# Routing attention with a hard-swish feed-forward: 32x32 block turns on VectorE for the sorted pairs

## Chip, core and metric

One Trainium2 chip, one core. The metric is device time in microseconds of one launch. All engines work on their own instruction streams and wait for each other through semaphores: TensorE (PE: matmuls and transposes by matmul), VectorE (DVE), ScalarE (ACT), GpSimd (POOL, which here also issues the gathers and scatters by row index) and SyncE (SP, which issues most transfers). Each engine runs its stream strictly in order, so an instruction that waits holds everything behind it on its engine.

## What is computed

```python
q_assign = argmax(q_n . c_n)          # per token and head, 16 clusters
k_assign = argmax(k_n . c_n)
mask = q_assign[:, :, :, None] == k_assign[:, :, None, :]
scores = scale * matmul(q, k.T);  scores = where(mask, scores, -1e9)
attn = softmax(scores);  x = matmul(attn, v)          # (4, 8, 768, 64)
x = x.transpose(0, 2, 1, 3).reshape(3072, 512)
h = x @ w_in                                          # 512 -> 2048
out = (h * clip(h + 3, 0, 6) / 6) @ w_out             # 2048 -> 512
```

Everything is float32; 4 batches, 8 heads, 768 tokens, head dimension 64.

## The kernel before, in words

Heads are handled in pairs, 16 of them (`NPAIR`), four to a batch. Pairs 0 to 6 take the plain way: all 768x768 scores with a mask added by a matmul. While they run, the weights are loaded and decoded by ACT and DVE, and the first eight items of the feed-forward are slipped in at the steps listed in `up_at`. Two steps `n` (a double step) are done per turn of that loop. The first feed-forward block needs `divide(0, 0)` (L529 to L533): the attention output `xb` times the reciprocal row sums `rb`, both fetched from DRAM.

Pairs 7 (`FIRST`) to 15 take the sorted way. For each pair g:

1. `load_natural` (L994) and `load_queries` (L997) fetch keys and queries in their natural order; `turn_natural` (L1023) turns them, so that the head dimension lies on partitions (`xnat`).
2. `cluster_scores`, `own_clusters`, `run_up`, `step_up`, `order`, `positions` find each token's place when tokens are sorted by cluster.
3. `scatter` (L1132) writes query rows (`qd`) and key and value rows (`kvd`) to DRAM at these places: 12 indirect transfers of 128 rows for the queries, 12 for keys and values, all issued by POOL, each followed by three tiny memsets (`pause`, L1128).
4. `load_ranked` (L1006) fetches the sorted rows; `turn_ranked` (L1029) turns queries and keys (`xsort`).
5. `band_scores`, `band_values`, `key_adds`, `band_sums`, `band_divide` do the attention in a band round the diagonal; `keep_ranked` writes the result in sorted order.
6. `gather` (L1176) brings the rows back to natural order: 12 indirect transfers on POOL; `turn_back` (L1328) turns them and writes them to the feed-forward's input `xd`.

A turn is `turn_piece` (L1016): six TensorE transposes of 128x128 into the PSUM tile `ps`, and one ScalarE copy of 128x768 back to SBUF.

The order of all this is written out by hand. `steps_of` (L1344) gives each step of a pair an offset; pair g's offset 0 lies at point `AHEAD + SLOT * (g - SECOND)` of one long list (`AHEAD` 38, `SLOT` 28, `SECOND` is pair 8). At each point its steps are issued, pair by pair in rising order, and then one half item of the feed-forward is taken from `fill` (`fill.pop(0)()`), but for offsets 6 and 9 of a slot. A feed-forward block (256 tokens) has 30 half items: 16 "up" (two for each of eight column groups, lines 710, 721, 540, 543, 700 in the profile) and 14 "down" (line 749). A batch has three blocks, 90 half items; a batch's items come into `fill` when its last pair has been turned back. So the last three blocks can only start after pair 15's `turn_back`.

Buffers that matter: `piecep` has two buffers for a loaded piece, `fromp` one each for the naturally ordered queries and for keys with values, `sortp` one shared by `xnat` and `xsort`, `psum_s` one.

```python
    SLOT, AHEAD = 28, 38
            busy = i >= AHEAD and (i - AHEAD) % SLOT in (6, 9)
            if fill and not busy:
                fill.pop(0)()
```

Of the kernel before, what the change touches and what calls it, by code (L numbers as in the profile page):

```python
# [8 lines left out]
F32 = mybir.dt.float32  # L9
# [7 lines left out]
B, H, S, D = 4, 8, 768, 64  # L17
C = 16
P = 128
NCH = S // P  # L20
# [105 lines left out]
def fast_path(ctx, tc, ok, q, k, v, centroids, moe_w_in, moe_w_out, out):  # L126
# [3 lines left out]
    nc = tc.nc  # L130
# [53 lines left out]
    st = {}  # L184
    later = []
# [225 lines left out]
    def where(n):  # L411
        g, r = divmod(n, 2 * NCH)
        return (g, *divmod(r, NCH))
# [34 lines left out]
    def key_sums(n):  # L448
        g, hf, j = where(n)
        ex = st["ex", n]  # L450
        if j == 1:
            acc = st["acc", g, hf] = accp.tile([P, 2, HALF], F32, name="acc")
            eng = nc.vector if WRITING[0] <= n < up_at[0] else nc.gpsimd
            eng.tensor_tensor(out=acc, in0=st["ex", n - 1], in1=ex, op=ALU.add)
        elif j > 1:
            acc = st["acc", g, hf]
            nc.gpsimd.tensor_tensor(out=acc, in0=acc, in1=ex, op=ALU.add)  # L457
        if hf == 1 and j == NCH - 1:
            st.pop(("xf", g)), st.pop(("xm", g))
# [47 lines left out]
    def load_sums(b):  # L507
        size = 2 * NCH
        tok = plain[:, NKT * b * size : (NKT * b + unsorted(b)) * size]
        nc.sync.dma_start(tok, st["sums", b].rearrange("k t s -> (k t s)").rearrange("(p n) -> p n", p=P))  # L510

        def invert():
            nc.vector.reciprocal(out=tok, in_=tok)
            nc.sync.dma_start(st["rd", b].rearrange("k t s -> (k t s)").rearrange("(p n) -> p n", p=P), tok)
            return complete

        def complete():
            if unsorted(b) == NKT:
                waiting.extend((b, m) for m in range(NHC))
                load_block()  # L520
            if b == 0:
                later.append(lambda: divide(0, 0))

        if b == 0:
            later.append(lambda: later.append(invert()))
        else:
            st["invert"], st["complete"] = invert, complete

    def divide(b, m):  # L529
        if ("rb", b, m) in st:  # L530
            xb, rb = st["xb", b, m], st.pop(("rb", b, m))
            kts = slice(0, unsorted(b))
            nc.vector.tensor_tensor(out=xb[:, kts], in0=xb[:, kts], in1=rb[:, kts], op=ALU.mult)  # L533
# [449 lines left out]
    def natural(x, g):  # L983
        b, h = divmod(2 * g, H)
        return x[b, h : h + 2].rearrange("t (p j) d -> p j t d", p=P)

    def ranked(name, g, t, part=0):
        return rows[name, g, t].rearrange("(i p) d -> p i d", p=P)[:, :, part * D : (part + 1) * D]

    def new_piece(key):  # L990
        piece = st[key] = st["piecep"].tile([P, NCH, 2, D], F32, name="piece")
        return piece

    def load_natural(g):  # L994
        nc.sync.dma_start(new_piece(("knat", g)), natural(k, g))

    def load_queries(g):  # L997
        qn = st["qn", g] = st["fromp"].tile([P, NCH, 2, D], F32, name="qn")
# [6 lines left out]

    def load_ranked(g, a):  # L1006
        if a < 2:
            piece = new_piece(("qk"[a] + "s", g))
            for t in range(2):
                nc.sync.dma_start(piece[:, :, t], ranked(("qd", "kvd")[a], g, t))  # L1010
            return
        vs = st["vs", g] = st["svp"].tile([P, 2, NCH, D], F32, name="vs")
        for t in range(2):
            nc.sync.dma_start(vs[:, t], ranked("kvd", g, t, 1))

    def turn_piece(piece, dst):  # L1016
        pt = st["psum_s"].tile([P, 2, 512], F32, name="ps")
        for i in range(NCH):
            at = i % NHC * P
            nc.tensor.transpose(out=pt[:, i // NHC, at : at + P], in_=piece[:, i], identity=ident)  # L1020
        nc.scalar.copy(out=dst.rearrange("p (h i) c -> p h (i c)", h=2), in_=pt[:, :, 0:HALF])

    def turn_natural(g, a):  # L1023
        if a == 1:
            st["xf", g] = st["sortp"].tile([P, NC2, P], F32, name="xnat", tag="x")
        piece = st.pop(("knat", g)) if a else st["qn", g]
        turn_piece(piece, st["xf", g][:, a * NCH : (a + 1) * NCH])

    def turn_ranked(g, a):  # L1029
        if a == 0:  # L1030
            st["xs", g] = st["sortp"].tile([P, NC2, P], F32, name="xsort", tag="x")
        turn_piece(st.pop(("qk"[a] + "s", g)), st["xs", g][:, a * NCH : (a + 1) * NCH])

    def own_clusters(g):
        st.pop(("xf", g))
# [303 lines left out]
            load_block()  # L1339
            fill.extend(ffn_items(b))  # L1340

    SLOT, AHEAD = 28, 38

    def steps_of(g):  # L1344

        first, last = g == SECOND, g == NPAIR - 1
        f = -3 if first else -5
        if first:
            plan = [
                (-38, load_queries), (-37, load_keys, 0), (-36, load_keys, 1), (-37, run_up),  # L1350
                (-36, step_up), (-31, order), (-30, positions),
            ]
        elif g == FIRST:
            plan = [(-7, lambda g: st.pop("signed")())]
        else:
            plan = [
                (-45, load_natural), (-41, load_queries), (-38, turn_natural, 1), (-37, turn_natural, 0),
                (-36, cluster_scores), (-34, own_clusters), (-33, run_up), (-32, step_up),
                (-30, load_keys, 0), (-29, order), (-29, positions), (-27, load_keys, 1),
            ]  # L1360
        s = -29 if first else -24
        if g == FIRST:
            plan += [(-9, load_ranked, 0), (-6, load_ranked, 1), (-5, load_ranked, 2), (-6, band_masks)]
        else:
            plan += [
                (s, scatter, 0), (s, scatter, 1), (-12, band_masks), (-11, load_ranked, 0), (f, load_ranked, 1),
                (f + 1, load_ranked, 2),
            ]
        plan += [(-1, turn_ranked, 0), (0, turn_ranked, 1)]
        d = 1 if last else 2  # L1370
        plan += [
            (d, band_scores, (0, 5), 1), (d + 2, band_scores, (2,), 3), (d + 4, band_scores, (4,)),
            (d + 4, band_values, 0), (d + 4, key_adds, 0, 1, 2), (d + 5, key_adds, 0, 3), (d + 7, band_values, 1),
            (d + 7, key_adds, 1, 1, 2), (d + 8, key_adds, 1, 3), (d + 10, band_sums),
            (12 if last else 14, band_divide), (14 if last else 16, keep_ranked),
            (15 if last else 23, gather), (28 if last else 37, turn_back),
        ]
        return [(g, *step) for step in plan]

    def late_plan():  # L1380
# [39 lines left out]
    decode += [lambda i=i: weight_sums(i) for i in range(4)]  # L1420
    st["kept"] = set()
    sooner = {0: 7, 2: 6, 4: 5, 6: 4}
    up_at = (60, 64, 70, 72, 76, 80, 82, 84)
    WRITING = (42, 84)

    def share(n, r):
# [21 lines left out]
    }  # L1448
    for n, part in ((36, 0), (40, 1), (52, 2), (62, 3), (68, 4), (74, 5)):
        ranking.setdefault(n, []).append(lambda part=part: early_rows(part))  # L1450
    writes = [lambda i=i: early_scatter(i) for i in range(4 * NCH)]

    HOLD = 6
# [16 lines left out]
    with tc.manual_schedule():  # L1470
# [24 lines left out]
        for n in range(0, total + lag_d + 2, 2):  # L1495
            g, r = divmod(n, per_pair)
            steps = [i for i in (n, n + 1) if i < total]
            prep = prep_items(g + 1, r)
            for i in steps:
                scores(i)  # L1500
                exponentials(i)
                key_sums(i)
            for i in (n - lag_v, n - lag_v + 1):
                if 0 <= i < total:
                    attn_v(i)
            m = n - lag_d + 1
            if m >= 0 and m % per_pair == per_pair - 1:
                sum_up(m // per_pair)
                ready(m)
            if WRITING[0] <= n < WRITING[1]:  # L1510
                for _ in range(2 if n < up_at[0] and n % NCH == 0 else 1):
# [411 lines left out]
```

## Time and profile before

| | us |
|---|---|
| median of 3 runs | 926.83 (926.22 to 930.19) |
| the profiled execution, own time | 930.95 |
| its span, first to last instruction | 929.2 |
| mean granted TensorE clock in it | 0.996 |

The profile's page gives, for each engine, the busy time, and the span in 40 slices (a digit is the busy share of a slice in tenths). Views of the trace name instructions by line, engine, operation and tiles ("out<-in"), with a start in microseconds from the span's start and a duration. "Idle before" is the time for which the engine stood still ahead of an instruction, with what ended it. PE matmuls overlap in the pipeline, so the time that a matmul takes from the stream is the distance from its start to the start of the next one, and not its shown duration.

The span has three parts. Up to some 217 us run the plain pairs; from there to some 766 us the sorted pairs, with feed-forward items between their steps; after that the rest of the feed-forward alone.

### The profile page before, as it was taken

The numbers are of one execution on the slowest core, as the hardware profiler recorded it, in microseconds if no ns is written. First come the engines' busy times: TensorE is split into PE (matmuls) and PEld (weight loads), VectorE is DVE, ScalarE is ACT, GpSimd is POOL, SyncE is SP. The second block draws the span as 40 slices with busy tenths as digits, with TensorE's granted clock in tenths as the row PEclk, the third lists the DMA queues.
The fourth block names the chain that finished last, engine by engine and source line by source line (L and its number), as shares of the span: only waits on it lengthen the run. The fifth ranks groups of instructions, "written<-read, shape, count | busy, mean of one in ns | idle before, by whom it ended". The sixth has DMA issues, their size and how long they took to land.

```text
span 929.2 us, 17674 instructions
## 1 busy us (share of the span) xinstructions
PE 912.7 (98%) x6323; PEld 722.1 (78%) x6323; DVE 563.0 (61%) x1341; ACT 329.7 (35%) x659; POOL 600.2 (65%) x1438
## 2 busy tenths in 40 slices
PE   8999989999999999999999999999999999999997
PEld 5444435557888798897887988988888899999996
DVE  6775877799785474493483572673571655536361
ACT  6888765761232332232232241331422311112120
POOL 3878897896487787788778787787887061203030
PEclk9999998999999999999999999999999999999999
DMA  6755673634756475482772835755563324323220
GB/s 177 194 136 160 174 216 121 187 100 129 201 152 148 115 211 141 144 211 74 198 200 74 228 89 155 186 150 131 135 168 88 103 71 128 91 75 108 59 67 27
DMA packets 187113, 128.31 MB, mean 138 GB/s; under 512 B 145708, under 2 KB 164552, under 8 KB 187016
## 3 DMA queue, kind: packets, MB, share of 16 engines
q1 hardware_dynamic: 162904, 78.46, 32.2%
q10 hardware_dynamic: 13744, 34.44, 13.2%
q0 software_dynamic: 10368, 14.18, 4.9%
q8 instruction: 52, 0.85, 0.4%
q14 instruction: 45, 0.37, 0.1%
HBM read 97.07 MB, written 29.97 MB: 137 GB/s over the span
## 4 chain that ended last, share of the span: by engine, by line
PE 92%; DVE 3%; ACT 2%; DMA 1%; issue 1%; SPq 1%; POOL 0%; DVEq 0%; POOLq 0%; ACTq 0%
PE Y L749 18%; PE uY L710 16%; PE X L749 13%; PE uX L710 13%; PE ps L423 6%; PE pv L467 5%; PE pv L1268 3%; PE ps L1020 3%; PE ps L1211 3%; PE ph L658 3%; PE pv L1211 1%; PE pqk L337 1%; PE pcs L356 1%; DMA rb<-rd 1%; PE pd L1292 1%; PE ps L1309 1%
## 5 line engine op out<-in xcount | busy, mean ns | idle before, releaser
L1181 POOL DMA_INDIRECT xn<-xsd,pos x108 | 106.6, 987 | 50.8 <-DVE sx L721 26.3
L1130 POOL MEMSET unread<- 128x1 f32 x972 | 102.1, 105 | 37.6
L1138 POOL DMA_INDIRECT qd<-qn,pos x96 | 97.5, 1016 | 35.0 <-issue 17.0
L457 POOL TENSOR_TENSOR acc<-acc,ex 128x768 f32<-128x768 f32 x56 | 104.2, 1861 | 21.6 <-ACT ex L446 19.0
L700 POOL TENSOR_TENSOR g_sb<-g_sb 128x256 f32<-128x256 f32 x52 | 39.1, 772 | 115.3 <-DVE g_sb L543 114.3
L540 ACT ACTIVATE sx<-g_sb,half_c 128x512 f32<-128x512 f32 x88 | 63.7, 724 | 138.0 <-DVE g_sb L721 138.0
L1138 POOL DMA_INDIRECT kvd<-kvn,pos x96 | 96.8, 1008 | 21.8 <-issue 21.8
L756 DVE TENSOR_TENSOR y<-y,Y 128x256 f32<-128x256 f32 x47 | 19.8, 420 | 126.3 <-PE Y L749 125.5
L710 PE MATMUL uX<-xb,w_in_sb 128*128 128x128 f32 x704 | 93.0, 275 | 0.0
L749 PE MATMUL X<-w_out_sb,g_sb 128*128 128x256 f32 x384 | 90.3, 382 | 0.0
L749 PE MATMUL Y<-T,g_sb 128*128 128x256 f32 x384 | 88.0, 381 | 0.0
L749 PE MATMUL Y<-w_out_sb,g_sb 128*128 128x256 f32 x384 | 87.9, 380 | 0.0
L710 PEld LDWEIGHTS uX<-xb,w_in_sb 128*128 128x128 f32 x704 | 85.7, 192 | 0.0
L749 PEld LDWEIGHTS Y<-T,g_sb 128*128 128x128 f32 x384 | 72.0, 190 | 12.9 <-issue 3.4
L749 PEld LDWEIGHTS X<-w_out_sb,g_sb 128*128 128x128 f32 x384 | 70.9, 190 | 13.9 <-issue 4.0
L721 DVE TENSOR_TENSOR sx<-uX,sx 128x128 f32<-128x128 f32 x176 | 50.9, 289 | 49.9 <-ACT sx L728 46.7
L749 PEld LDWEIGHTS Y<-w_out_sb,g_sb 128*128 128x128 f32 x384 | 71.8, 190 | 10.4 <-issue 1.0
L423 PE MATMUL ps<-xf 64*128 64x384 f32 x336 | 68.8, 487 | 0.7 <-ACT ex L446 0.7
L721 DVE TENSOR_TENSOR g_sb<-uY,sx 128x128 f32<-128x128 f32 (+1 forms) x176 | 65.5, 413 | 0.0
L543 DVE SCALAR_TENSOR_TENSOR g_sb<-sx,g_sb 128x512 f32<-128x512 f32 x88 | 63.7, 726 | 2.6 <-ACT sx L540 2.5
L446 ACT ACTIVATE ex<-ps 128x768 f32<-128x768 f32 x84 | 63.7, 802 | 3.1 <-PE ps L423 2.6
L467 PE MATMUL pv<-ex,vt 128*64 128x384 f32 x336 | 63.5, 499 | 0.0
(232 smaller groups left out, 1769.7 us busy)
## 6 DMA issues: line engine op xcount, KB each, us to landing
tx<-td ACTq DMA_DIRECT2D x86, 384.0 KB
raw<-in_moe_w_in_dram SPq DMA_DIRECT2D x16, 512.0 KB
raw<-in_moe_w_out_dram SPq DMA_DIRECT2D x16, 512.0 KB
xb<-xd SPq DMA_DIRECT2D x12, 512.0 KB
out_dram<-y SPq DMA_DIRECT2D x44, 128.0 KB
piece<-qd SPq DMA_DIRECT2D x18, 192.0 KB
piece<-kvd SPq DMA_DIRECT2D x18, 192.0 KB
vs<-kvd SPq DMA_DIRECT2D x18, 192.0 KB
```

The lines of the kernel that those rows point to most:

```text
L423: nc.tensor.matmul(st["ps", n][:, t, 0:HALF], lhsT=x[r, NCH + j], rhs=x[r, hf * NHC : (hf + 1) * NHC], start=first, stop=last, skip_group_ ...
L446: nc.scalar.activation(out=ex, in_=sc, func=ACT.Exp, scale=SM_SCALE)
L457: nc.gpsimd.tensor_tensor(out=acc, in0=acc, in1=ex, op=ALU.add)
L467: nc.tensor.matmul(pv[t * D : (t + 1) * D], lhsT=vt[:, t, j], rhs=ex[:, t], start=(j == 0), stop=(j == NCH - 1),)
L540: nc.scalar.activation(out=r, in_=h, func=ACT.Relu, bias=half_c, scale=1.0 / 6.0)
L543: nc.vector.scalar_tensor_tensor(out=g, in0=r, scalar=1.0, in1=h, op0=ALU.min, op1=ALU.mult)
L710: nc.tensor.matmul(dst, lhsT=w[:, kt], rhs=x(kt), start=(kt == 0), stop=(kt == HK - 1))
L721: nc.vector.tensor_tensor(out=out_, in0=in0, in1=in1, op=ALU.add)
L749: nc.tensor.matmul(bank[:, half * HC : (half + 1) * HC], lhsT=g_sb[:, kind, i], rhs=w[:, i], start=(first and i == 0), stop=(last and i == ...
L1130: nc.gpsimd.memset(unread, 0.0)
L1138: i = nc.gpsimd.indirect_dma_start(out=rows[name, g, t], in_=src[:, j, t].rearrange("p a d -> p (a d)") if a else src[:, j, t], in_offset= ...
L1181: nc.gpsimd.indirect_dma_start(out=xn[:, j, t], out_offset=None, in_=rows["xsd", g, t], in_offset=bass.IndirectOffsetOnAxis(ap=pos[:, 0, j ...
```

## The change

It touches three things.

*The turns.* Queries and keys of the sorted pairs are loaded as 32x32 blocks, so that each block of 32 tokens by 32 dimensions stands on 32 partitions; one VectorE transpose of 128x768 (which turns each 32x32 block in place) then gives the same layout as six TensorE transposes and a ScalarE copy gave. Each load becomes four transfers of 32 partitions by 24 runs of 32 floats (128 bytes). The naturally ordered queries are now loaded twice, once as blocks for the turn and once as rows for the scatter. `turn_back` and `band_divide` stay with TensorE.

*The order.* `SLOT` goes from 28 to 29; natural loads, the row load of the queries and the load of the sorted queries move to other offsets; the last pair's steps move closer together.

*The start of the feed-forward.* The first two of the eight early items move from steps 60 and 64 to 64 and 68, and `divide(0, 0)` is issued at step 60 from the list `ranking`.

```diff
-    def load_natural(g):
-        nc.sync.dma_start(new_piece(("knat", g)), natural(k, g))
+    def load_natural(g, a):
+        b, h = divmod(2 * g, H)
+        blocks = new_blocks(("nat", g, a))
+        for t in range(2):
+            rows_ = (q, k)[a][b, h + t].rearrange("(r j c) (x i) -> x j c r i", j=Q, c=NCH, i=Q)
+            for x in range(2):
+                at = (2 * t + x) * Q
+                nc.sync.dma_start(
+                    blocks[at : at + Q].rearrange("p (c r i) -> p c r i", c=NCH, i=Q), rows_[x]
+                )
+
+    def load_sorted(g, a):
+        blocks = new_blocks(("sorted", g, a))
+        for t in range(2):
+            rows_ = rows[("qd", "kvd")[a], g, t].rearrange("(b j) (x i) -> x j b i", j=Q, i=Q)
+            for x in range(2):
+                at = (2 * t + x) * Q
+                nc.sync.dma_start(blocks[at : at + Q].rearrange("p (b i) -> p b i", i=Q), rows_[x])
+
+    def turn_blocks(piece, dst):
+        nc.vector.transpose(out=dst.rearrange("p j c -> p (j c)"), in_=piece)
...
-        piece = st.pop(("knat", g)) if a else st["qn", g]
-        turn_piece(piece, st["xf", g][:, a * NCH : (a + 1) * NCH])
+        turn_blocks(st.pop(("nat", g, a)), st["xf", g][:, a * NCH : (a + 1) * NCH])
...
-        turn_piece(st.pop(("qk"[a] + "s", g)), st["xs", g][:, a * NCH : (a + 1) * NCH])
+        turn_blocks(st.pop(("sorted", g, a)), st["xs", g][:, a * NCH : (a + 1) * NCH])
...
-    SLOT, AHEAD = 28, 38
+    SLOT, AHEAD = 29, 38
...
-                (-45, load_natural), (-41, load_queries), (-38, turn_natural, 1), (-37, turn_natural, 0),
+                (-44, load_natural, 1), (-43, load_natural, 0), (-38, turn_natural, 1), (-37, turn_natural, 0),
+                (-34, load_queries),
...
-                (s, scatter, 0), (s, scatter, 1), (-12, band_masks), (-11, load_ranked, 0), (f, load_ranked, 1),
+                (s, scatter, 0), (s, scatter, 1), (-12, band_masks), (-7, load_ranked, 0), (f, load_ranked, 1),
...
+        if last:
+            plan += [
+                (1, band_scores, (0, 5), 1), (2, band_scores, (2,), 3), (3, band_scores, (4,)),
+                (3, band_values, 0), (3, key_adds, 0, 1, 2), (4, key_adds, 0, 3), (5, band_values, 1),
+                (5, key_adds, 1, 1, 2), (6, key_adds, 1, 3), (8, band_sums), (9, band_divide), (10, keep_ranked),
+                (11, gather), (22, turn_back),
+            ]
...
-    up_at = (60, 64, 70, 72, 76, 80, 82, 84)
+    up_at = (64, 68, 70, 72, 76, 80, 82, 84)
...
+    ranking[60] = [lambda: divide(0, 0)]
```

For the last pair, `band_divide`, `gather` and `turn_back` stood at offsets 12, 15 and 28 before and stand at 9, 11 and 22 now; for all others they keep 14, 23 and 37.

More of the change, by code (lines that the diff above doesn't have):

```diff
@@ L452, in key_sums @@
             acc = st["acc", g, hf] = accp.tile([P, 2, HALF], F32, name="acc")
-            eng = nc.vector if WRITING[0] <= n < up_at[0] else nc.gpsimd
+            eng = nc.vector if WRITING[0] <= n < 60 else nc.gpsimd
             eng.tensor_tensor(out=acc, in0=st["ex", n - 1], in1=ex, op=ALU.add)
@@ L520, in complete @@
                 load_block()
-            if b == 0:
-                later.append(lambda: divide(0, 0))
         if b == 0:
@@ L988, in ranked, with new_blocks @@
         return rows[name, g, t].rearrange("(i p) d -> p i d", p=P)[:, :, part * D : (part + 1) * D]
-    def new_piece(key):
-        piece = st[key] = st["piecep"].tile([P, NCH, 2, D], F32, name="piece")
-        return piece
-    def load_natural(g):
-        nc.sync.dma_start(new_piece(("knat", g)), natural(k, g))
+    Q = 32
+    def new_blocks(key):
+        piece = st[key] = st["piecep"].tile([P, S], F32, name="piece")
+        return piece
+    def load_natural(g, a):
[17 more added lines that the diff above has]
+        nc.vector.transpose(out=dst.rearrange("p j c -> p (j c)"), in_=piece)
     def load_queries(g):
@@ L1007, in load_ranked @@
         if a < 2:
[L1008 to L1011, printed above, removed]
+            return load_sorted(g, a)
         vs = st["vs", g] = st["svp"].tile([P, 2, NCH, D], F32, name="vs")
@@ L1369, in steps_of @@
         plan += [(-1, turn_ranked, 0), (0, turn_ranked, 1)]
[L1370 to L1377, printed above, removed]
+        if last:
[5 more added lines that the diff above has]
+            ]
+        else:
+            plan += [
+                (2, band_scores, (0, 5), 1), (4, band_scores, (2,), 3), (6, band_scores, (4,)),
+                (6, band_values, 0), (6, key_adds, 0, 1, 2), (7, key_adds, 0, 3), (9, band_values, 1),
+                (9, key_adds, 1, 1, 2), (10, key_adds, 1, 3), (12, band_sums), (14, band_divide), (16, keep_ranked),
+                (23, gather), (37, turn_back),
+            ]
         return [(g, *step) for step in plan]
@@ L1510, in fast_path @@
             if WRITING[0] <= n < WRITING[1]:
-                for _ in range(2 if n < up_at[0] and n % NCH == 0 else 1):
+                for _ in range(2 if n < 60 and n % NCH == 0 else 1):
                     writes.pop(0)()
```

## The prediction, made before the run

> **What bounds the kernel now.** I read the page's totals first, then the waits of PE, then POOL's groups and its order of time.
>
> ```profile
> PE 912.7 (98%) x6323; PEld 722.1 (78%) x6323; DVE 563.0 (61%) x1341; ACT 329.7 (35%) x659; POOL 600.2 (65%) x1438
> POOL 3878897896487787788778787787887061203030
> ```
>
> PE is busy for 98% of the span, so time taken off PE's stream counts, as long as nothing else steps forward. POOL's 65% misleads: its row of slices is dense up to the 31st of the 40 and nearly empty behind. PE's waits are few:
>
> ```profile
> PE ph L658 <- DVE xb L533: 4.6, 1, 4.6
> PE pd L1292 <- DVE bw L1282: 0.8, 1, 0.8
> ```
> Each row gives the total in us, how often, and the longest. Two windows of 6 us at that place show the busy time of PE, PEld, DVE, ACT and POOL, then the granted clock, the DMA share and GB/s:
>
> ```profile
> 134.00:140.00 6.00, 2.69 (x18) 0.95 (x14) 1.41 (x1) 1.40 (x5) 5.65 (x7) 0.98 0.97 284
> 140.00:146.00 6.00, 4.74 (x11) 3.82 (x12) 5.83 (x7) 2.54 (x6) 5.46 (x10) 0.50 0.11 24
> ```
>
> The one large wait is the first feed-forward item's, for `divide(0, 0)`; behind it the clock stands at 0.50 for 6 us. So this wait costs 4.6 us and then half of the 4.74 us that PE was busy in the second window, 2.4 us: 7.0 us.
>
> Now POOL in the sorted part, first its groups (busy us, mean ns, then idle time before them), then four of its instructions in order of time (start, duration):
>
> ```profile
> L1181 POOL DMA_INDIRECT xn<-xsd,pos x108 | 106.6, 987 | 50.8 <-DVE sx L721 26.3 <-issue 11.6 <-ACT sx L728 0.7
> L1130 POOL MEMSET unread<- 128x1 f32 x972 | 102.1, 105 | 37.6
> L1138 POOL DMA_INDIRECT qd<-qn,pos x96 | 97.5, 1016 | 35.0 <-issue 17.0 <-DVE tx L600 16.7 <-DVE g_sb L721 1.3
> L1138 POOL DMA_INDIRECT kvd<-kvn,pos x96 | 96.8, 1008 | 21.8 <-issue 21.8
> ```
> ```profile
> 243.34 0.99 POOL L1138 DMA_INDIRECT qd<-qn,pos  x1 [16.70 <-DVE tx L600]
> 244.92 0.97 POOL L1138 DMA_INDIRECT qd<-qn,pos  x1 [0.16 <-issue]
> 280.39 1.01 POOL L1138 DMA_INDIRECT kvd<-kvn,pos  x1 [0.16 <-issue]
> 697.82 0.97 POOL L1138 DMA_INDIRECT kvd<-kvn,pos  x1 [0.16 <-issue]
> ```
>
> One indirect transfer with its pauses takes 1.58 us, and but for two waits (16.7 us before the first, 26.3 us before the last gather) POOL waits for nobody: it works without a break from 243.34 to 698.79 us, 455.5 us, to the end of pair 15's scatter. From pair 8's last scatter (ends 281.40) to pair 15's (698.79) are seven pairs: 59.6 us each. PE's pace is read from its turns:
>
> ```profile
> 298.51 0.82 PE L1020 MATMUL ps<-ident,piece 128*128 128x128 f32 x6
> 299.17 0.24 PE L1089 MATMUL rk<-every,upto 128*128 128x1 bf16 x4
> ...
> 706.31 0.82 PE L1020 MATMUL ps<-ident,piece 128*128 128x128 f32 x6
> 706.97 1.89 PE L749 MATMUL Y<-w_out_sb,g_sb 128*128 128x256 f32 x8
> 708.70 0.82 PE L1020 MATMUL ps<-ident,piece 128*128 128x128 f32 x6
> 709.35 0.81 PE L749 MATMUL Y<-T,g_sb 128*128 128x256 f32 x3
> ```
>
> Pair 8's first sorted turn starts at 298.51 and pair 15's at 706.31: 58.3 us per pair. So two streams are full side by side, PE at 58.3 and POOL at 59.6 us per pair; PE starts with a lead of work and POOL eats into it. This is where I expect most of the saving to be lost.
>
> **The change part by part.** *Turns off PE.* From a turn's start to the next instruction are 299.17 - 298.51 = 0.66 us. The trace has:
>
> ```profile
> L1020 PE MATMUL ps<-ident,piece 128*128 128x128 f32 x150 | 20.6, 274 | 0.1
> L1020 PE MATMUL ps<-ident,qn 128*128 128x128 f32 x42 | 5.7, 273 | 0.0
> ```
>
> 192 transposes, 32 turns: 32 x 0.66 = 21.1 us off PE. ACT loses 32 copies, which matters little at 35%.
>
> *The early wait.* In the changed order six more decoding steps stand before `divide(0, 0)` on DVE, and the items that need it come a double step later, so the 7.0 us should go. If only PE counted, the span would be 929.2 - 21.1 - 7.0 = 901.1 us.
>
> *Turns onto DVE.* No DVE transpose is in this trace. The nearest rows for 768 elements:
>
> ```profile
> L1200 DVE TENSOR_SCALAR xmsort<-places,ends 128x768 bf16<-128x768 int16 x9 | 3.9, 429 | 0.0
> L454 DVE TENSOR_TENSOR acc<-ex 128x768 f32<-128x768 f32 x3 | 3.7, 1223 | 2.3 <-ACT ex L446 2.3
> ```
> and three windows, an up stretch beside sorted steps, a whole block alone, and that block's down stretch:
>
> ```profile
> 450.50:480.80 30.30, 30.17 (x273) 28.94 (x273) 24.32 (x78) 9.92 (x20) 24.47 (x73) 1.00 0.80 209
> 775.50:824.60 49.10, 49.10 (x337) 46.23 (x336) 23.48 (x61) 8.08 (x18) 8.47 (x12) 1.00 0.30 87
> 800.60:824.60 24.00, 24.00 (x113) 21.13 (x112) 6.86 (x16) 1.47 (x3) 1.48 (x3) 1.00 0.13 42
> ```
>
> 0.43 us (2-byte data) and 1.22 us (float32, two inputs); I take 0.95, nearer to the float32 row: 30 us of DVE in all. The worst stretch for it is an up stretch with four turns in it, such as 450.5 to 480.8 us: there DVE is busy for 24.3 us, would be for 28.1 (29.2 at the upper bound), and PE's work falls from 30.2 to 27.5. So DVE is over by 0.6 to 1.7 us, in some five such stretches, and PE now meets DVE at 16 joins (a turn's result is read one or two items later): I allow 2 us net.
>
> VectorE: DVE Perf Modes in the Trainium skill (sections "The three transpose paths" and "Rules for kernel authors") speaks against this part: it advises TensorE for a 128x128 transpose whose result may land in PSUM, and gives 311 ns for 128x128 of bf16 in 32x32 blocks on VectorE. An estimate from that page's figure is 6 x 311 ns = 1.87 us a turn, twice what I take; no run here shows it yet. By it the stretch above would be over by 24.3 + 4 x 1.87 - 27.5 = 4.3 us, 21 us in five; less the 4 hidden in step 3 and the 2 allowed, the median would come to as much as 927.
>
> *Transfers.* A block load is 4 x 32 x 24 = 3072 packets. 14 natural loads take the place of 7 with 1536, and 18 sorted ones of 1536 now have 3072: 59,904 packets more.
>
> ```profile
> q1 hardware_dynamic: 162904, 78.46, 32.2%
> 347.00:360.00 13.00, 13.00 (x78) 11.53 (x78) 8.91 (x28) 1.89 (x3) 10.43 (x33) 1.00 0.95 220
> L995 SPq DMA_DIRECT2D piece<-in_k_dram x7: 607/620/1006, 247.6 to 616.8; - x7
> ```
>
> The queue's mean is 0.322 x 16 x 929.2 / 162904 = 29 ns, so at most 12% more of the 16 engines' time, where single stretches stand at 0.95 already. SP issues 85 more transfers at 0.6 us, some 2.4 us a load. The loads have five or six points (10 us at 58.3 / 28) until their turn: hidden, except for the last sorted keys.
>
> *`SLOT` 29.* A half item is 49.10 / 30 = 1.64 us. PE's pace becomes 58.3 - 4 x 0.66 + 1.64 = 57.3 us a pair against POOL's 59.6: PE loses 2.3 us of lead per pair, where it lost 1.4. So the end is set by POOL from about pair 13 on.
>
> *The chain that follows POOL.* Its rows:
>
> ```profile
> 693.34 7.08 SPq L1010 DMA_DIRECT2D piece<-kvd  x2
> ...
> 737.13 0.49 PE L1305 MATMUL pdt<-ident,dn 128*128 128x128 f32 x3
> 744.78 0.94 POOL L1181 DMA_INDIRECT xn<-xsd,pos  x1 [26.30 <-DVE sx L721]
> 762.48 0.94 POOL L1181 DMA_INDIRECT xn<-xsd,pos  x1
> 764.44 0.82 PE L1020 MATMUL ps<-ident,xn 128*128 128x128 f32 x6
> 768.45 0.54 SPq L579 DMA_DIRECT2D xb<-xd  x1
> 772.88 0.42 DVE L634 TENSOR_TENSOR xs<-xb 128x256 f32<-128x256 f32 x1 [2.37 <-DMA xb<-xd]
> 775.46 0.61 PE L710 MATMUL uX<-xs,tx 128*128 128x128 f32 x4
> ```
>
> 1. POOL's first scatter follows `positions(8)`: 243.34 - 7.0, and one DVE transpose (0.95) now stands ahead of it: 237.3. Stream 455.5: pair 15's scatter ends at 692.8.
> 2. Its keys: the second load's issue ended at 700.42, 1.6 after the scatter; one issue more 0.4; landing 2.5 (estimate: below the 4.4 from 768.45 to 772.88 for a larger load); transpose 0.95. First band scores at 698.2.
> 3. To `band_divide`: 709.35 to 737.13 is 27.8 us with ten half items; now seven: 22.9, so 721.1. PE's own sum, with five more items issued by then, is 737.13 - 28.1 + 8.2 = 717.2; POOL decides by 4 us.
> 4. To `turn_back`: 737.13 to 764.44, 27.3 us, in which the twelve gathers alone take 18.6. PE now has 12 items there, 20.7 us with the divide's transposes, and stands still for 6.6 us; for the clock behind that, as after the early wait, 1 us: 749.4.
> 5. To the last three blocks: 11.0 before; the data path (768.45, 772.88) is 9.5, one item less stands between; with 1 us of slow clock 10.5: 759.9.
> 6. From there 775.46 to 929.2, 153.7 us: 913.6. With the 2 us at the joins (the 4 us of step 3 hides the rest): span 915.
>
> That is 14 us less than the profiled execution's span (929.2, own time 930.95). That execution lies 4.1 us above the median of the runs; 14.5 off the median gives 912.
>
> **The rivals.** *POOL gets out of the way* (an earlier start, keys landing at once): then 901.1 and the 6.6 us of step 4 remain, 907.7, median 905. For it: POOL's lead at pair 8 is 17 us. Against it: its stream has no gap left. *DVE becomes the bound*: transposes at the upper bound, so 1.7 us over in five stretches, and a lag of 1 us at each of the 16 joins, 24.5 us; less the 4 hidden and the 2 allowed, 18.5, of which I take half as made good in down stretches: median 921. For it: 24.3 of 30.3 us busy; against: the down stretch that follows has DVE busy for 6.9 of 24 us. VectorE: DVE Perf Modes in the Trainium skill ("Rules for kernel authors") points the same way. *Blocks land late*: DVE waits at a turn for 128-byte packets, in order, with every feed-forward add behind it, and PE stands after it. The place is the 16 pairs of turns; it decides from (14.5 + 4 + 4.6) / 16 = 1.4 us per join on; at 3 us it gives 912 + 48 - 6 = 954, at 2 us 938. For it: the 0.95 share; against: a margin of 10 us. DMA: Bandwidth & Descriptors in the Trainium skill ("Specifications") asks for transfers of 512 bytes or more for line rate, which speaks for this rival; no run here shows what it costs. *The early wait only moves* (`rb` lands no sooner): 7 us back, 919.
>
> **How the numbers follow.** POOL's chain 0.60, POOL out of the way 0.14, DVE the bound 0.10, blocks late 0.10, early wait kept 0.06. The forecast is 912. The range runs from 902, a little under the second case, to 923 above the DVE case; it leaves out the late blocks. Half a per cent (4.6 us) is about what a measurement of this kernel can tell from no change: faster means under 922.2, all of the forecast and the second case, the early wait and part of the DVE case: 0.83; same 0.09, slower 0.08, from late blocks.
>
> **What would show it.** A wait of PE near 134 to 141 us and a clock of 0.50 there would refute the early part. DVE transposes should last 0.95 us. POOL should start near 237 and run gapless, with DVE or PE waiting for `piece<-kvd` in the last pairs and PE idle 5 us or more before the last `turn_back`, at a half clock behind. If POOL's scatters end near 693 and PE has no wait, the chain is wrong; so it is if DVE waits for `piece<-in_q_dram` throughout.

## The result, and the profile after

| | before | after |
|---|---|---|
| median, same chip | 928.73 us (926.22 to 931.74, 6 runs) | 954.89 us (953.25 to 955.67, 6 runs) |
| ratio after / before | | 1.0275 (95%: 1.0253 to 1.0296) |
| span of the profiled execution | 929.2 us | 951.4 us |

The changed kernel is 2.75% slower; 912 us had been forecast. Its page, with the mean granted clock of the view by core (code lines have moved: the new turn is L1014, the scatter L1153, the gather L1196, the band scores L1226, the feed-forward L708 and L747):

```profile
core 0: 951.4 us, clock 0.983
PE 903.6 (95%) x6131; PEld 706.6 (74%) x6131; DVE 587.6 (62%) x1373; ACT 305.3 (32%) x627; POOL 601.4 (63%) x1438
PE 70%; DVE 17%; DMA 5%; POOL 3%; issue 2%; ACT 2%; SPq 1%; ACTq 0%; DVEq 0%; POOLq 0%
```

The second row says where the 22.2 us of span come from. PE's busy time fell from 912.7 to 903.6, by 9.1 us, though 21.1 us of turns were taken off it: 12.0 us were given back, because PE ran slower. The clock says the same: 951.4 x 0.017 = 16.2 us lost to it after, 929.2 x 0.004 = 3.7 before. And PE's time outside its work grew from 16.5 to 47.8 us, by 31.3. Then -9.1 + 31.3 = 22.2. The third row, the chain of work that ended last, gives DVE 17% of it where it had 3%.

PE's waits (total us, times, longest us), with the groups of the new turn (minimum, median and maximum ns) from the view of its line:

```profile
PE pcs L356 <- DVE xnat L1014: 13.8, 7, 3.2
PE ps L1226 <- DVE xsort L1014: 7.3, 5, 2.9
PE ps L423 <- ACT ex L446: 5.0, 3, 4.4
PE ps L1036 <- DMA xn<-xsd,pos: 4.1, 4, 1.3
PE X L747 <- DVE g_sb L541: 2.9, 3, 1.8
```
```profile
L1014 DVE STREAM_TRANSPOSE xsort<-piece x18: 933/970/980, 242.0 to 735.2; 128x768 f32<-128x768 f32 x18
L1014 DVE STREAM_TRANSPOSE xnat<-piece x14: 958/969/971, 285.4 to 662.8; 128x768 f32<-128x768 f32 x14
its engine sat idle before it (us, times) until:
who waited for it (us, times):
```

The first two rows are the joins: in 12 of 16, PE stood for the DVE turn whose result it reads next, 21.1 us in all (by chance the figure of the turns that were taken off PE). Of the 31.3 us, the remaining 10 are mostly the last gathered rows and the feed-forward. The second view has an empty list under "its engine sat idle before it": DVE never waited for a block load. It came late because of its own queue. One join in order of time, DVE and then PE (start, us; the time in brackets is the wait):

```profile
346.04 1.55 DVE L698 TENSOR_TENSOR g_sb<-g_sb 128x256 f32<-128x256 f32 x4
347.51 0.97 DVE L1014 STREAM_TRANSPOSE xnat<-piece 128x768 f32<-128x768 f32 x1
348.40 0.58 DVE L719 TENSOR_TENSOR sx<-uX,sx 128x128 f32<-128x128 f32 x2
348.90 0.97 DVE L1014 STREAM_TRANSPOSE xnat<-piece 128x768 f32<-128x768 f32 x1
```
```profile
346.06 0.61 PE L708 MATMUL uY<-xs,w_in_sb 128*128 128x128 f32 x4
349.92 1.51 PE L356 MATMUL pcs<-xnat,cnT 128*32 128x384 f32 x8 [3.25 <-DVE xnat L1014]
```

PE had finished its items at about 346.7. DVE, busy without a break, still had a gated product (L698) from the half item before, then two turns with another half item's sums between them, and was through at 349.9. What follows is the second price. The same place in windows (busy us of PE, PEld, DVE, ACT and POOL, then the clock, DMA share and GB/s):

```profile
345.00:350.00 5.00, 1.75 (x19) 1.56 (x22) 4.90 (x12) 0.87 (x2) 3.75 (x11) 0.92 0.78 238
350.00:356.00 6.00, 6.00 (x19) 3.83 (x20) 3.51 (x9) 1.10 (x2) 4.49 (x16) 0.50 0.97 190
```

PE works through 350 to 356 at half clock, which makes 3 us of work take 6. Of five such stretches after, three follow joins (at 349, 414 and 557 us), one the wait at 142 us and one the wait for the last gathered rows at 783.

The wait that the early part was to remove is still there, under another name:

```profile
140.50 0.66 ACT L245 ACTIVATE wsize<-raw 128x512 bf16<-128x512 f32 x1 [5.02 <-DMA raw<-in_moe_w_out_dram]
141.16 1.49 ACT L446 ACTIVATE ex<-ps 128x768 f32<-128x768 f32 x2
```
```profile
142.00 0.50 PE L423 MATMUL ps<-xm 64*128 64x384 bf16 x2 [4.36 <-ACT ex L446]
```
```profile
134.00:141.00 7.00, 3.61 (x24) 1.90 (x25) 4.31 (x7) 1.95 (x5) 6.52 (x7) 1.00 1.05 301
141.00:148.00 7.00, 6.00 (x23) 2.26 (x22) 6.79 (x9) 5.75 (x13) 6.29 (x10) 0.51 0.36 127
```

ACT stands 5.02 us for a piece of raw weights while the 16 DMA engines are full (1.05, 301 GB/s). The exponentials are queued behind that on ACT, and PE needs their score bank. The half clock behind it is the same as before. And ACT had stood still at this place in the kernel before too, at the same time as DVE's wait for `rb`, though there PE's wait was put down to `divide`:

```profile
139.53 0.66 ACT L245 ACTIVATE wsize<-raw 128x512 bf16<-128x512 f32 x1 [4.57 <-DMA raw<-in_moe_w_out_dram]
```

So two waits for the full DMA engines ended there within 1 us of each other, and taking away the one leaves the other.

POOL, finally: its first and its last sorted scatter, and its waits ahead of the scatters.

```profile
244.35 1.00 POOL L1153 DMA_INDIRECT qd<-qn,pos  x1 [17.53 <-DVE pos L1136]
```
```profile
720.85 0.97 POOL L1153 DMA_INDIRECT kvd<-kvn,pos  x1 [0.15 <-issue]
```
```profile
POOL qd L1153 <- DVE pos L1136: 30.5, 5, 17.5
```

The stream starts at 244.35, not 237, and ends at 721.82, not 692.8: 477.5 us in place of 455.5. Of the 30.5 us, 17.5 lie ahead of the first scatter, where it waited 16.70 before too; 13.0 are new, for positions that come late, since `positions` stands behind the natural join. Another 10.4 us ahead of scatters are put down to the sums on DVE (`sx`, L719).

### The profile page after: what moved, and what is told of

Read it like the earlier page. It is cut to its first block, busy times and chain, and to the rows that moved or that the text cites. A ratio compares the mean times of both kernels' runs of the same rounds, so it can differ in the third digit from the quotient of the medians.

```text
span 951.4 us, 17419 instructions
## 1 busy us (share of the span) xinstructions
PE 903.6 (95%) x6131; PEld 706.6 (74%) x6131; DVE 587.6 (62%) x1373; ACT 305.3 (32%) x627; POOL 601.4 (63%) x1438
## 3 DMA queue, kind: packets, MB, share of 16 engines
q1 hardware_dynamic: 224168, 81.22, 35.2%
## 4 chain that ended last, share of the span: by engine, by line
PE 70%; DVE 17%; DMA 5%; POOL 3%; issue 2%; ACT 2%; SPq 1%; ACTq 0%; DVEq 0%; POOLq 0%
PE Y L747 15%; PE uY L708 11%; PE X L747 10%; PE uX L708 8%; PE ps L423 6%; PE pv L467 5%; PE pv L1283 3%; PE ps L1226 3%; POOL xn L1196 2%; DVE g_sb L541 2%; DVE g_sb L698 2%; DVE sx L719 2%; PE ph L656 2%; PE pv L1226 1%; DVE g_sb L719 1%
## 5 line engine op out<-in xcount | busy, mean ns | idle before, releaser
L1196 POOL DMA_INDIRECT xn<-xsd,pos x108 | 107.3, 993 | 49.8 <-DMA xsd<-xr 26.8
L1153 POOL DMA_INDIRECT qd<-qn,pos x96 | 97.4, 1014 | 54.6 <-DVE pos L1136 30.5
L698 POOL TENSOR_TENSOR g_sb<-g_sb 128x256 f32<-128x256 f32 x52 | 39.5, 781 | 118.1 <-DVE g_sb L541 117.1
L1153 POOL DMA_INDIRECT kvd<-kvn,pos x96 | 96.0, 1000 | 21.4 <-issue 21.4
L747 PE MATMUL X<-w_out_sb,g_sb 128*128 128x256 f32 x384 | 96.1, 397 | 2.9 <-DVE g_sb L541 2.9
L708 PE MATMUL uX<-xb,w_in_sb 128*128 128x128 f32 x704 | 93.0, 275 | 0.0
L747 PE MATMUL Y<-w_out_sb,g_sb 128*128 128x256 f32 x384 | 89.3, 384 | 0.0
L747 PE MATMUL Y<-T,g_sb 128*128 128x256 f32 x384 | 88.7, 381 | 0.0
L747 PEld LDWEIGHTS X<-w_out_sb,g_sb 128*128 128x128 f32 x384 | 74.0, 199 | 19.7 <-issue 4.6
L708 PEld LDWEIGHTS uX<-xb,w_in_sb 128*128 128x128 f32 x704 | 85.7, 192 | 0.0
L747 PEld LDWEIGHTS Y<-w_out_sb,g_sb 128*128 128x128 f32 x384 | 72.9, 192 | 11.8 <-issue 1.6
L747 PEld LDWEIGHTS Y<-T,g_sb 128*128 128x128 f32 x384 | 72.0, 190 | 11.8 <-issue 2.1
L719 DVE TENSOR_TENSOR sx<-uX,sx 128x128 f32<-128x128 f32 x176 | 50.7, 288 | 42.6 <-ACT sx L726 39.4
L719 DVE TENSOR_TENSOR g_sb<-uY,sx 128x128 f32<-128x128 f32 (+1 forms) x176 | 65.5, 413 | 0.0
```

Source lines behind the costliest of these rows:

```text
L708: nc.tensor.matmul(dst, lhsT=w[:, kt], rhs=x(kt), start=(kt == 0), stop=(kt == HK - 1))
L719: nc.vector.tensor_tensor(out=out_, in0=in0, in1=in1, op=ALU.add)
L747: nc.tensor.matmul(bank[:, half * HC : (half + 1) * HC], lhsT=g_sb[:, kind, i], rhs=w[:, i], start=(first and i == 0), stop=(last and i == ...
L1153: i = nc.gpsimd.indirect_dma_start(out=rows[name, g, t], in_=src[:, j, t].rearrange("p a d -> p (a d)") if a else src[:, j, t], in_offset= ...
L1196: nc.gpsimd.indirect_dma_start(out=xn[:, j, t], out_offset=None, in_=rows["xsd", g, t], in_offset=bass.IndirectOffsetOnAxis(ap=pos[:, 0, j ...
```

## The experiments

15 kernels ran. Ratios are to the kernel before on the same chip, with 95% intervals; spans, clock and PE's busy time are those of each profiled execution.

| kernel | median us | ratio | span | clock | PE busy |
|---|---|---|---|---|---|
| e1_early_alone | 928.95 | 0.9991 (0.9974 to 1.0007) | 927.3 | 0.998 | 910.8 |
| e2_order_alone | 937.18 | 1.0068 (1.0041 to 1.0095) | 936.3 | 0.995 | 913.3 |
| e3_natural_apart | 936.11 | 1.0072 (1.0046 to 1.0098) | 934.0 | 0.990 | 898.8 |
| e4_both_apart | 932.79 | 1.0026 (1.0010 to 1.0042) | 931.9 | 0.994 | 895.7 |
| e5_apart_pool | 1186.78 | 1.2770 (1.2734 to 1.2806) | 1185.2 | 0.895 | 959.9 |
| e6_before_pool | 1166.46 | 1.2518 (1.2491 to 1.2546) | 1171.7 | 0.897 | 997.4 |
| e7_plain_loads | 958.32 | 1.0317 (1.0281 to 1.0353) | 958.2 | 0.981 | 907.3 |
| e8_after_pool | 1168.86 | 1.2616 (1.2577 to 1.2656) | 1163.5 | 0.901 | 972.3 |
| e9_no_meeting | 926.81 | 0.9971 (0.9950 to 0.9992) | 925.3 | 0.994 | 895.5 |
| e10_last_later | 931.39 | 1.0010 (0.9987 to 1.0033) | 930.2 | 0.992 | 895.0 |
| e11_slot_28 | 919.25 | 0.9884 (0.9846 to 0.9921) | 918.3 | 0.995 | 893.3 |
| e12_pool_longer | 962.96 | 1.0362 (1.0325 to 1.0400) | 959.8 | 0.980 | 905.0 |
| e13_after_28 | 959.34 | 1.0267 (1.0211 to 1.0323) | 963.1 | 0.981 | 909.9 |
| e14_best_no_early | 924.23 | 0.9900 (0.9866 to 0.9934) | 926.1 | 0.995 | 896.6 |
| e15_apart_28 | 928.12 | 0.9950 (0.9916 to 0.9984) | 918.9 | 0.996 | 892.9 |

**The early part alone.** The kernel before with only the first half items moved and `divide(0, 0)` issued from the list.

```diff
+    ranking[60] = [lambda: divide(0, 0)]
-    up_at = (60, 64, 70, 72, 76, 80, 82, 84)
+    up_at = (64, 68, 70, 72, 76, 80, 82, 84)
```

> The kernel before with only the early part of the change: first two feed-forward items at steps 64 and 68, divide(0, 0) at step 60. The step of the prediction: 7 us gone, median near 921. Theory that the wait only changes hands (ScalarE is held at the same moment by a weight load that shares the full DMA queues): no change, 927 to 931, with a wait of PE of over 4 us near 142 us and a clock of 0.5 behind it.

Worth nothing that can be measured, and PE's wait again changed hands:

```profile
PE ps L423 <- ACT ex L446: 4.7, 5, 3.7
```

**The order alone.** The kernel before with pairs 29 points apart and the last pair's steps as after; turns stay on TensorE.

```diff
-    SLOT, AHEAD = 28, 38
+    SLOT, AHEAD = 29, 38
```

> The kernel before with SLOT 29 and the closer steps of the last pair; turns stay on TensorE. Theory O (the new order costs the time): 945 or more. Theory J (the cost is at the joins, where PE reads a turn that VectorE has not reached): near before, 927 to 937, the upper end if PE stands still for 6 us ahead of the last turn_back and at half clock behind it.

0.7% slower: PE waits 1.8 us for `tx` and 2.5 us for the last gathered rows, with a stretch of half clock behind. So this part of the order has a price of its own, some 6 us, but far from the whole 26. The moved loads are not in this kernel.

**The natural joins moved apart.** The changed kernel, with the natural blocks loaded and turned three points earlier, so that five half items and not two lie between the first turn and the read.

```diff
-                (-44, load_natural, 1), (-43, load_natural, 0), (-38, turn_natural, 1), (-37, turn_natural, 0),
+                (-47, load_natural, 1), (-46, load_natural, 0), (-41, turn_natural, 1), (-40, turn_natural, 0),
```

> The changed kernel with the natural loads and turns three points earlier, so that five points lie between a turn and cluster_scores' first read instead of two and one. Theory J: the 13.8 us that PE waits for xnat vanish, and two of the stretches at half clock (5 us): median near 936. Theory P (the 59,904 packets more of 128 bytes slow the transfers) and theory O: within 3 us of the changed kernel, 952 to 958.

The ratio went from 1.0275 to 1.0072, some 19 us, for four numbers in a list, and the median is the 936 us that the theory of the joins had given. Its waits of PE:

```profile
PE ps L1226 <- DVE xsort L1014: 7.9, 5, 3.1
PE ps L1036 <- DMA xn<-xsd,pos: 4.1, 4, 1.3
PE X L747 <- DVE g_sb L541: 4.0, 4, 1.8
```

The row of `xnat`, 13.8 us before, is gone; `xsort`, which was not touched, stays.

**Both joins moved apart.** In addition the band scores come four points after the second sorted turn where they came two points after it.

```diff
-                (2, band_scores, (0, 5), 1), (4, band_scores, (2,), 3), (6, band_scores, (4,)),
+                (4, band_scores, (0, 5), 1), (6, band_scores, (2,), 3), (8, band_scores, (4,)),
```

(the following steps up to `band_sums` likewise, `band_divide` and `keep_ranked` by one point; the last pair's steps, its gather and turn back too, by one point)

> As e3_natural_apart, and the band attention two points later (one for the last pair), so that xsort has time too. Theory J: the 7.3 us of waits for xsort and one more stretch at half clock (3.4 us) vanish as well: near 925. Theories P and O: 950 or more.

```profile
PE ps L1226 <- ACT xt L1037: 6.2, 7, 0.9
PE X L747 <- DVE g_sb L541: 4.1, 5, 1.8
PE ps L1036 <- DMA xn<-xsd,pos: 2.8, 3, 1.4
```

Both joins are gone from the list, but the time missed the 925 expected by 8 us. The first row is a new meeting: offset 8 is also where the previous pair's `turn_back` lies (37 - 29), and `psum_s` has one buffer.

**The packets.** The changed kernel with plain transfers under the same VectorE turns. Its turned tiles then hold other blocks, so that its clusters and scores are of other data; every instruction stays.

```diff
-            rows_ = rows[("qd", "kvd")[a], g, t].rearrange("(b j) (x i) -> x j b i", j=Q, i=Q)
-            for x in range(2):
...
+            nc.sync.dma_start(
+                blocks.rearrange("p (j t d) -> p j t d", j=NCH, t=2)[:, :, t],
+                ranked(("qd", "kvd")[a], g, t),
+            )
```

(the natural loads likewise)

> The changed kernel with its transfers as they were (rows of 64 elements instead of blocks of 32 by 32) under the same turns on VectorE: the turned tiles then hold the wrong blocks, so the clusters and scores are of other data; every instruction stays. Theory J (TensorE reads a turn one or two items after VectorE, which is behind): the packets cost nothing, 951 to 957 us as the changed kernel. Theory P (the 59,904 packets more crowd the queues): 930 to 940 us.

Not faster at all; the waits at the joins are there in full. The queue's packets fell from 224,168 to this:

```profile
q1 hardware_dynamic: 173992, 81.22, 32.6%
PE pcs L356 <- DVE xnat L1012: 15.2, 7, 3.3
PE ps L1224 <- DVE xsort L1012: 8.2, 5, 2.9
```

The kernel thus takes back some 50,000 of the 59,904 packets that the change added (the natural queries are still loaded twice), and these cost nothing that shows. The theory of late blocks falls.

**POOL's pauses, one instead of three.** Meant to lift POOL's stream out of the way, in three kernels: the version with both joins apart, the kernel before, and the changed one.

```diff
-    PAUSE = 3
+    PAUSE = 1
```

> The kernel of e4_both_apart (turns on VectorE, both joins moved apart) with one memset behind each indirect transfer on POOL in place of three. Asked: why e4_both_apart, in which TensorE has 21 us less to do and waits little for VectorE, is still not faster than the kernel before. Theory F (floor): POOL's stream without gaps, from the first scatter of the first pair to the last scatter of the last, and the chain of the last pair behind it set the end; 300 transfers of that stretch with two memsets less each shorten it by tens of us, so the end then goes by TensorE: 910 to 920 us. Rival J2: it is still the waits of TensorE and the halved clock, at other places; then POOL's share is worth nothing and the time stays within 4 us of e4_both_apart's 932.8.

> The kernel before with one memset behind each indirect transfer in place of three: the control of e5_apart_pool. Theory F says that before, TensorE had work enough to follow POOL with few gaps (10.6 us idle in all, 6.6 of it ahead of the last turn_back), so that at most these 6.6 us and the slow clock behind them can go: 921 to 929 us. If POOL alone sets the end of this kernel too, it falls by tens of us.

> The changed kernel with one memset behind each indirect transfer in place of three. Theory J: VectorE's lag at the joins is independent of POOL; the 24.8 us of waits and 8.6 us of halved clock stay, and only what POOL's stream adds at the end (4.1 us of wait for the last gather and 3.4 us of halved clock behind it) goes: 944 to 951 us. If the late positions (30.5 us of POOL waiting for VectorE) were the cause of the slowdown through POOL, it falls to 925 to 935 us.

All three missed by far, and say nothing on their question: they are 25 to 28% slower than the kernel before. The kernel before, first as it was, then with one memset, in two windows each:

```profile
245.00:268.00 23.00, 23.00 (x199) 19.26 (x198) 14.85 (x39) 8.71 (x18) 18.72 (x57) 1.00 0.61 170
285.00:300.00 15.00, 15.00 (x86) 12.61 (x85) 5.64 (x20) 1.43 (x3) 12.10 (x39) 1.00 0.41 84
```
```profile
245.00:268.00 23.00, 7.66 (x31) 5.49 (x28) 1.54 (x5) 0.27 (x1) 19.55 (x38) 0.61 0.26 77
285.00:300.00 15.00, 15.00 (x136) 14.26 (x136) 12.63 (x36) 4.11 (x9) 0.72 (x1) 1.00 0.49 127
```

With one memset POOL's first sorted scatter goes on until 268 us. In it PE is busy for a third of the time, where it was busy throughout before; DVE, ACT and the DMA engines do even less. When POOL pauses (0.72 us busy in 15) PE is back at full pace. More on this at the end.

**The meeting removed, and the last turn later.** First `turn_back` two points later in the version with both joins apart, then the last pair's three points later too.

```diff
-                (23, gather), (37, turn_back),
+                (23, gather), (39, turn_back),
...
-                (12, gather), (23, turn_back),
+                (12, gather), (26, turn_back),
```

> The kernel of e4_both_apart with the turn back of a pair 2 points later (39 for 37), so that its score bank is no longer asked for at the point at which the next pair's band scores ask for it: the seven waits of ps<-xmsort for ACT xt (0.89 us each, 6.2 us) go. Asked: what still holds e4_both_apart at 932.8 us. Theory W (small waits of TensorE, each with a cause of its own): the 6.2 us come off, 925 to 928 us. Theory F (POOL's stream from the first scatter to the last and the chain behind it are the floor): the waits turn up elsewhere, 930 to 934 us.

> e9_no_meeting with the last pair's turn back 3 points later (26 for 23): TensorE's two waits for the last gathered rows (2.5 us) and half of the 3.4 us at half clock behind them go. Theory W: 4 us below e9_no_meeting, 921 to 925 us. Theory F: no lower than e9_no_meeting.

The first came as the theory of single waits has it: 6.6 us less in span, that `xt` row gone. The second missed: 4.6 us more. The wait for the rows went, and a larger one came behind it:

```profile
764.02 1.89 PE L747 MATMUL Y<-T,g_sb 128*128 128x256 f32 x8
774.59 1.22 PE L708 MATMUL uX<-xs,tx 128*128 128x128 f32 x4 [8.67 <-DVE xs L632]
```

After the last turn PE has one half item left before it needs the next blocks, which come from that very turn, through DRAM and back. `fill` is empty.

**28 points again, and POOL made longer.** Both edit the version with the last turn later.

```diff
-    SLOT, AHEAD = 29, 38
+    SLOT, AHEAD = 28, 38
```
```diff
-    PAUSE = 3
+    PAUSE = 4
```

> e10_last_later with pairs 28 points apart as before, instead of 29: a pair then holds 2 us of TensorE's work less than POOL's 59 us, so that TensorE must wait for POOL's rows or the positions if POOL's stream is a floor. Theory F: slower than e10_last_later by 3 to 12 us, with waits of TensorE for transfers behind POOL. Theory W without a floor: within 3 us of e10_last_later.

> e10_last_later with a fourth memset behind each indirect transfer on POOL: some 0.14 us more for each of 300 transfers, up to 42 us on POOL's stream between the first scatter and the last. Theory F (the stream sets the end): 35 to 45 us slower than e10_last_later. Theory W: POOL has room at each pair, and less than 10 us arrive.

28 points were expected to cost or do nothing, and gave 12 us: 919 us, faster than the kernel before. The place of the last turn shows why:

```profile
750.16 0.82 PE L1036 MATMUL ps<-ident,xn 128*128 128x128 f32 x6
750.81 3.62 PE L747 MATMUL Y<-w_out_sb,g_sb 128*128 128x256 f32 x16
...
764.63 0.61 PE L708 MATMUL uX<-xs,tx 128*128 128x128 f32 x4
```

Each pair takes one half item less out of `fill`, so 13.8 us of items now lie between the turn and the blocks that it feeds, where there were 1.9 us of items and a wait of 8.67. And POOL still counts: DVE waits in this run 9.4 us for the last `piece<-kvd` (the scatter's rows), PE 3.2 us behind it. The fourth memset made the way from the first sorted scatter to the end of the last one 496.1 us long where it was 457.3, 38.8 us more, and the time 31.6 us longer: less than the 35 to 45 expected, but four fifths of what was added arrive. So a longer stream of POOL reaches the end almost in full, as in the forecast's chain. That a shorter one would bring the end forward is not shown by any run, and the 7 us that did not arrive may be room that the stream had.

**Undoing parts at the end.** The changed kernel with 28 points and nothing else; the 919 us version without the early part; and both joins apart with 28 points, without the later turns back.

> The changed kernel with pairs 28 points apart as before, instead of 29, and nothing else undone. Theory J (the joins with VectorE's turns carry the loss): each join stays where it is, so most of the loss stays, 940 to 952 us. Theory S (the distance of 29 points carries it, as the 12 us between e10_last_later and e11_slot_28 suggest): 920 to 935 us.

> e11_slot_28 with the early part of the change undone (the first half's divide and first items at their old points). By e1_early_alone, where this part alone was worth nothing: within 4 us of e11_slot_28's 919 us. If the early wait's 4.4 us and 6.9 us at half clock now decide differently: 5 us or more away.

> e4_both_apart with 28 points: both joins apart, the turns back where the changed kernel has them (37 falls on the next pair's point 9, not 8, so that the score bank's meeting is gone by the distance alone). Theory S with J: e11's gain is the two together, 918 to 924 us. If the later turns back in e11_slot_28 had a share: 925 us or more.

The first keeps the whole loss by its ratio (1.0267 against 1.0275), more than the 940 to 952 us expected, though on this chip the kernel before took 933.75 us: with the joins where they are, PE stands at them whatever lies between pairs.

```profile
PE pcs L356 <- DVE xnat L1014: 13.4, 5, 5.4
PE ps L1226 <- DVE xsort L1014: 11.9, 4, 3.3
```

The second is 5 us above the 919, but on a chip on which the kernel before was 3.7 us above its other median; by the ratios (0.9900 against 0.9884, intervals overlapping) the early part has no share that can be measured. The third was at 0.9950, with runs from 920.71 to 936.19 us on a chip on which the kernel before also went from 929 to 937. It is faster than the kernel before; whether it is behind the 919 us version, the intervals, which just overlap, do not settle. Its median lies where a share of the later turns back had been expected.

## Why the prediction was wrong

- *Turns off PE, 21.1 us.* Right. With the joins apart PE's busy time is 893 to 899 us; in the quickest version 893.3, which is 19.4 below 912.7.
- *0.95 us for a DVE transpose.* Right: 0.97 us, and never idle ahead of it. The estimate from VectorE: DVE Perf Modes in the Trainium skill ("The three transpose paths"), 6 x 311 ns = 1.87 us, is twice what the trace shows.
- *"I allow 2 us net" at the 16 joins.* This is the step that failed. The waits at the joins are 21.1 us, ten times that, and half clock behind three of them adds to it (17.1 us of it by the granted clock of the trace, so an estimate of 8.5 us); moving only the natural joins took 19 us off the time, moving both 23 (from a ratio of 1.0275 to 1.0026, of 929). The text had the parts: two turns follow each other, a half item's sums stand between them, PE reads one or two items later, and DVE is busy for 24.3 of 30.3 us there. But the excess was averaged over a stretch of 30 us, while what PE meets is DVE's queue at one instant: 1.55 + 2 x 0.97 + 0.58 us at 346 to 350. The rival "DVE becomes the bound" named the mechanism, priced it at a lag of 1 us a join and took half as made good later. Single waits were up to 3.2 us, the clock behind them was not in it, and nothing of it shows as made good: PE's time outside its work grew by 31.3 us.
- *The early wait, "so the 7.0 us should go".* Wrong; the rival "the early wait only moves" was right, though its reason was only near it. `raw`, on ACT, came late, and not `rb`. The forecast read only the one of the two waits in the trace before; ACT's 4.57 us stood beside it.
- *Packets hidden.* Right, shown by the run with plain loads for most of them. DMA: Bandwidth & Descriptors in the Trainium skill ("Specifications") asks for 512 bytes or more for line rate; the 128-byte packets here had no cost that shows, with a margin of some 10 us ahead of most turns.
- *POOL's chain.* Step 1 was wrong for the changed kernel: 244.35, as the early wait stayed, and a stream that waited 30.5 us. The premise was that PE keeps ahead of POOL. Where the joins are apart it holds nearly: the stream takes 453 to 463 us in those runs. In the last run of the table POOL's first and last sorted scatters are

```profile
237.59 0.99 POOL L1153 DMA_INDIRECT qd<-qn,pos  x1 [16.71 <-DVE pos L1136]
```
```profile
691.86 0.97 POOL L1153 DMA_INDIRECT kvd<-kvn,pos  x1 [0.16 <-issue]
```

  against 237.3 and an end at 692.8 in the forecast, and the span is 918.9 against 915. So close an agreement is in part luck: this execution is the quickest of ten with a median of 928.12 us. In it the wait near 140 us was only 1.7 us, with no half clock behind, and POOL starts some 6 us earlier than in the 919 us version (243.5).
- *PE idle 5 us or more before the last turn, half clock behind.* Idle 4.1 us, then half clock from 783 to 790: right in kind.
- *`SLOT` 29.* Its cost was read only from the pace of PE against POOL. That each pair takes one item more from those that cover the last pair's chain was not in the sum; with the joins apart and the last turn later it is worth 12 us, and 8 us against the run that has the last turn where it was (0.9971 to 0.9884). In the changed kernel itself it is worth nothing that can be measured (1.0267).

Open: the share of waits and of clock in the 22 us is from one profiled execution each.

## What to carry to other kernels

When work moves to an engine with time to spare, look at each place where the busy engine reads the result, list what stands in the other engine's queue at that instant, and put enough of the busy engine's own work between the two; the mean load of the engine says nothing about it. A short stand costs twice where the clock falls behind it. And work that can fill a gap is a stock: one item more per pair in the middle is missing at the end, where the last chain needs cover.

## What was not expected of the hardware

**The spacing of indirect transfers.** With three memsets (0.43 us) behind each, POOL issues one every 1.55 us, and PE was busy for 23.00 of 23 us; with one, every 1.28 us, it was busy for 7.66. The loss builds up: POOL began at 237.50 us, PE was still busy for 9.91 of the 10 us from 237 to 247, and after POOL's last instruction at 268 PE stayed slow for some 4 us more (0.95 of 4 us busy). The largest of PE's waits in that kernel name no engine:

```profile
PE uY L710 <- issue: 56.0, 58, 2.2
PE uX L710 <- issue: 23.9, 28, 2.9
```

"issue" is time in which the engine waited for nothing that the profile shows. So the rest of the core keeps up with one transfer in 1.55 us and not with one in 1.28. What is short there, and where between the two it begins, is not shown by any run; 0.28 us saved on each of 324 transfers (91 us of POOL's own time) cost the kernel before 238 us.

**The clock's fall depends on when a wait falls, not only on its length.** A stand of 2.33 us at a join in the run with the natural joins apart was followed by 3.4 us at half clock; one of 3.22 us in the 919 us version was not, nor was one of 2.99 us in the changed kernel (at 538.6 us):

```profile
239.00:242.50 3.50, 1.17 (x8) 0.53 (x9) 3.43 (x8) 0.00 (x0) 0.82 (x1) 0.99 0.38 148
242.50:246.00 3.50, 3.50 (x16) 2.09 (x13) 0.94 (x3) 1.71 (x3) 2.93 (x10) 0.53 0.37 136
```
```profile
698.50:702.30 3.80, 0.58 (x6) 0.23 (x6) 1.17 (x2) 0.00 (x0) 3.11 (x12) 1.00 0.81 170
702.30:706.00 3.70, 3.70 (x32) 2.78 (x34) 0.57 (x3) 1.95 (x4) 3.06 (x9) 1.00 0.78 191
```

TensorE: Matmul & The Clock Gate in the Trainium skill ("What's actually happening") states that the clock is set over a window of about 3.4 us that runs freely, so that the moment of change varies. The stretches at half clock in the runs with three memsets, 3.4 or 6.8 us each, agree with that. Its table has the clock fall after an idle window of that length; this does not agree, since a stand of 2.33 us, with PE busy for 1.17 of the 3.5 us, was enough.
